# A fifth weight buffer for the experts, loaded during attention, and contiguous pieces of w3

## The chip, the cores and the metric

One core of a Trainium2 chip runs the kernel. The metric is the device time of one execution in microseconds (us), the median of several runs.

## The reference, cut to what matters

```python
attn_out = _attn_ref(q, k, v)          # 8 batches, 8 heads, 576 positions, 64 wide, mask by blocks of 64
x = attn_out.transpose(0, 2, 1, 3).reshape(4608, 512)
# soft mixture of 8 experts, 4 slots each
logits = x @ phi                        # 4608 x 32
d = softmax(logits, axis=0); slot_input = (d.T @ x).reshape(8, 4, 512)
for e in range(8):
    slot_out[e] = np.maximum(slot_input[e] @ w1[e], 0) @ w2[e]     # 512 -> 1024 -> 512
x = softmax(logits, axis=1) @ slot_out.reshape(32, 512)
# gated layer, its four weights in float64
h = (x @ m2_w1) * (x @ m2_w2) @ m2_w3   # 512 -> 1024, 1024 x 1024
out = h @ m2_w_out                      # 1024 -> 512
```

## The kernel before

**Attention** (class `Attn`) works through 32 pairs of heads. Each pair has a set of operands in one of four buffers ("set", L91-L98; in the orders below set_65 to set_68 are the buffers of pairs 0 to 3, and of 4 to 7 again). A set is made from a loaded q/k piece ("raw", 576 KB): for pairs 0 to 2 by `prep_first` (L161-L176, copies on DVE and ACT, two subtractions on POOL, L174 and L176), for all later ones by `prep_hi` (ACT copy L150) and `prep_lo` (POOL subtraction L158), with four moves by DMA (L179), three of them one after the other behind the subtraction. For each pair PE computes a first set of scores for the row maxima (`max_tile`, L191, tile "mx"), which DVE reduces (L195, L201); the maxima go through L225, L227 and a small product (`mrow`, L238) into the set. Then come the scores (`qk_unit`, L261, tile "sc"), their exponentials on ACT (L270 and L278, tiles PTa and PTb), the products with v (`pv`, L321) and the sums, for which POOL adds up exponentials (`preadd`, L294, tile "acc"). The maxima run two pairs ahead of the scores, the sets three. The word list `ORDER` gives the program order; a scheduler with its own model of times may reorder each engine's instructions, SP's (DMA issue) among them, and it does so in all of attention.

While attention runs, DVE turns the float64 bits of the gated layer's w1 and w2 into float32 (`narrow`, four instructions L627, L628, L629, L635; ACT helps with L631). Near its end, when a set is free for good, it becomes a window of 16 KB per partition, and `load_expert` (L657-L666) loads expert weights into it, 2 MB each; index i = 2e is w1 of expert e, i = 2e + 1 its w2.

**The experts** (`Rest.run`). SP's order is by hand here (`manual_schedule` for SP). First 17 pieces of 512 KB are issued: all eight of w_out and nine of the sixteen of w3. DVE converts the 24 pieces in a fixed order with the same four instructions each; ACT and POOL split each into a high and a low part (`split`, L669, L670). PE multiplies w3 by w_out from them: 192 matmuls "wps" (L725), 24 for each of eight row blocks, twelve for each half of w3's block; matmuls 13 to 24 need the ninth converted piece. Between these, for each expert, PE computes h (32 matmuls in groups, L805), transposes it (L822), ACT applies the relu (L823), and PE adds the product with w2 to "so" (L832). `w_steps` spreads loads, conversions and wps over the experts by the tables LOAD, CONV and MM. After the h of expert e, window i = 2e is loaded again with index 4 + 2e, after its so with 4 + 2e + 1 (L808 and L834 call `load_expert(NB + ...)`):

```python
        if i < NB:
            self.windows.append(self.keep["place"](i, F32, f"win{i}"))
        v = self.windows[i % NB][:, 0:4096].rearrange("p (c f) -> p c f", c=4 if first else 8)
```

**After them** come soT (L772), the products with the gated layer's w1 and w2 (L875), products of slots on DVE (L902 to L910), the matrix H (L924), and the last stage, in which PE makes 36 output tiles (L1029).

Of the kernel before, what the change touches and what calls it, by code (L numbers as in the profile page):

```python
# [7 lines left out]
F32 = mybir.dt.float32  # L8
# [8 lines left out]
NP_B = 4  # L17
NB = 4
RAW = 2
VB = 3  # L20
# [34 lines left out]
class Attn:  # L55
# [476 lines left out]
    def run(self):  # L532
# [31 lines left out]
        for n in range(N + 1):  # L564
            for t in (self.ORDER if n < N else self.LAST).split():
                k = int(t[1]) if t[1:].isdigit() else 0
                if t[0] == "M" and t != "MR":
                    self.max_tile(n + ML, k)
                elif t[0] == "Q":
                    self.qk_unit(n, int(t[1]), int(t[2]))  # L570
                    if N - NB <= n < N and t == "Q11" and self.after_scores:
                        self.after_scores(n - N + NB)
                elif t[0] == "V":
                    self.pv(n - 1, k)
                elif t[0] == "A":
                    self.preadd(n, k)
                elif t == "PH":
                    self.prep_hi(n + LA)
                elif t == "PL":
                    self.prep_lo(n + LA)  # L580
                elif t == "L2":
                    self.level2(n + ML)
                elif t == "MR":
                    self.mrow(n + ML)
                elif t == "SU":
                    self.sums(n - 1)
                elif t == "LD":
                    self.load(n + LA + 1)
                    self.load_v(n + VL)
                elif t == "PT":  # L590
                    if n and n % NP_B == 0:
                        self.push_tail(n // NP_B - 1)
                elif t == "T":
                    self.step(1)
                elif t == "BG":
                    if self.background and n >= 1 and (n == 1 or n * 16 // BGP > (n - 1) * 16 // BGP):
                        with self.tc.issue_after(self.last_max[n + 1]) if n < BGF else nullcontext(), self.tc.issue_after(self.last_exp[n - 1]):
                            self.background.popleft()()
# [5 lines left out]
class Rest:  # L604
# [3 lines left out]
    def __init__(self, tc, ctx, io, keep):  # L608
# [5 lines left out]
        self.wA, self.wB = (self.pre.tile([128, 4, 1024], F32, name=f"w{m}") for m in "AB")  # L614
        self.loaded, self.windows = deque(), []

# [40 lines left out]
    def load_expert(self, i):  # L657

        if i >= 16:
            return  # L660
        e, first = i // 2, i % 2 == 0
        if i < NB:
            self.windows.append(self.keep["place"](i, F32, f"win{i}"))
        v = self.windows[i % NB][:, 0:4096].rearrange("p (c f) -> p c f", c=4 if first else 8)
        self.nc.sync.dma_start(out=v, in_=self.io["moe_w1" if first else "moe_w2"][e].rearrange("(c p) f -> p c f", p=128))
        self.loaded.append(v)  # L666

# [4 lines left out]
    def run(self, out):  # L672
        nc, tc, io, keep = self.nc, self.tc, self.io, self.keep
        ident = keep["ident"]
        with ExitStack() as ctx:
# [9 lines left out]
            def load(i):  # L685
# [5 lines left out]
                else:  # L691
                    raw = w3_raw.pop((j, g)) if (j, g) in w3_raw else w3_tile(j, g)
                    src = io["w3T"][512 * g:512 * g + 512, 256 * j:256 * j + 256].rearrange("(c p) f -> p c f", p=128)
                    nc.sync.dma_start(out=raw.rearrange("p (c f) -> p c f", c=4), in_=src)
                raws[i] = raw
# [94 lines left out]
            hT = []  # L790
            for t in self.windows:
                t = t[:, 4096:8 * S]
# [3 lines left out]
            for e in range(8):  # L796
                hi = tc.high_priority() if HP else nullcontext()
                hi.__enter__()
                w = self.loaded.popleft()

                hp = ps.tile([128, 512], F32, tag="h", name="h", bufs=2)
                for dc in range(4):
                    for g in range(4):
                        with tc.issue_after(so_last) if 0 < e <= SEQ else nullcontext():
                            nc.tensor.matmul(hp[32 * g:32 * g + 32, 0:256], lhsT=siT[:, dc],  # L805
                                             rhs=w[:, dc, 256 * g:256 * g + 256], start=dc == 0, stop=dc == 3)
                self.load_expert(NB + 2 * e)
                if e == 5:  # L808
# [19 lines left out]
                hi.__enter__()  # L828
                w = self.loaded.popleft()
                for f in range(8):  # L830
                    g = f % 4
                    so_last = nc.tensor.matmul(so[32 * g:32 * g + 32], lhsT=hT[e][:, f], rhs=w[:, f],  # L832
                                               start=e == 0 and f < 4, stop=e == 7 and f >= 4).ins
                self.load_expert(NB + 2 * e + 1)  # L834
                hi.__exit__(None, None, None)
# [45 lines left out]
            for t in range(4):  # L881
                pe[0] = nc.tensor.transpose(p[:, 128 * t:128 * t + 128], abs_[:, 128 * t:128 * t + 128], ident).ins
            AB = mp.tile([128, 1024], F32, tag="hs", name="AB").rearrange("p (m f s) -> p m f s", m=2, f=8)
            AT, BT = AB[:, 0], AB[:, 1]
# [197 lines left out]
def layout(inputs):  # L1082
    import numpy as np

    f = np.float32
# [10 lines left out]
    vv[:, :, :512] = v[:, :, :512].reshape(N, 2, 4, 128, 64).transpose(0, 3, 2, 1, 4).reshape(N, 128, 512)  # L1096
    vv[:, :, 512:] = v[:, :, 512:].reshape(N, 128, 64)
    phi = inputs["moe_phi"]
    phib = np.zeros((128, 4, 64), f)
# [10 lines left out]
    for h in range(2):  # L1110
# [3 lines left out]
        for j in range(4):  # L1114
# [3 lines left out]
    return {"moe_w1": inputs["moe_w1"], "moe_w2": inputs["moe_w2"], "moe2_w1": inputs["moe2_w1"],  # L1118
            "moe2_w2": inputs["moe2_w2"], "w3T": np.ascontiguousarray(inputs["moe2_w3"].T),
            "w_out": inputs["moe2_w_out"], "sel32": sel32,  # L1120
# [23 lines left out]
```

## Time and profile before

| | |
|---|---|
| median of 3 runs | 670.13 us (667.66 to 670.2) |
| the profiled execution | 670.19 us |
| its span, first to last instruction | 668.3 us |
| mean granted clock of TensorE | 0.971 |
| PE busy | 620.1 us (93%), 4423 matmuls |
| DVE, ACT, POOL busy | 459.6, 349.2, 365.0 us |
| DMA | 141.45 MB, 212 GB/s over the span |

How to read it: PE, DVE, ACT and POOL are the four computing engines, PEld is PE's weight load, SPq is the queue that issues the DMAs. In a timeline a line has the start, the time until the last of its instructions ends, engine, source line, operation, what is written from what, how many, and in brackets the idle time before the first with what ended it. In a table of stretches each engine has its busy time and the number of instructions; then come the granted clock (1.00 is full), the DMA engines' busy share and GB/s.

### The profile page before, as it was taken

Reading aid. Unit: us, or ns where it says so; the run is one execution under the profiler, and the core shown is the slowest. Engines: PE = TensorE matmul, PEld = TensorE weight load, DVE = VectorE, ACT = ScalarE, POOL = GpSimd, SP = SyncE. Lnnn points to the kernel's source line nnn. Section 1 sums busy time; section 2 is a strip of 40 time slices with the busy share of each in tenths; the row PEclk is TensorE's granted clock in tenths of the full one; section 3 lists DMA queues with packets and bytes.
Section 4 is the critical chain, followed back from the end, with each engine's and each line's share of the span. In section 5 each row is a group of like instructions: output and inputs, shape, how many; then the busy total and the mean of one; then the engine's idle time right before and its main releaser. Section 6 shows DMA issues by size and latency. Waiting matters only on the chain. (4 is left out here: it accounts for less than half of the span.)

```text
span 668.3 us, 11772 instructions
## 1 busy us (share of the span) xinstructions
PE 620.1 (93%) x4423; PEld 450.7 (67%) x4423; DVE 459.6 (69%) x813; ACT 349.2 (52%) x645; POOL 365.0 (55%) x312
## 2 busy tenths in 40 slices
PE   4689989999999999999999997869999979999997
PEld 2666667777777777777777755426664667888886
DVE  6745829778867888687885656899923998555450
ACT  6855537475655657476664543335424345444541
POOL 8856838778677877877785650244414332123320
PEclk9978979999999999999999998979999997999999
DMA  6597687777788878788866679999893404655742
GB/s 210 145 221 198 156 227 180 183 231 173 208 223 213 214 189 225 183 214 219 224 164 198 214 282 338 330 385 400 320 343 109 130 12 131 211 181 188 252 150 94
DMA packets 59640, 141.45 MB, mean 212 GB/s; under 512 B 5928, under 2 KB 23848, under 8 KB 59560
## 3 DMA queue, kind: packets, MB, share of 16 engines
q1 hardware_dynamic: 59404, 140.63, 70.8%
q8 instruction: 35, 0.57, 0.4%
q14 instruction: 21, 0.17, 0.1%
q10 hardware_dynamic: 180, 0.07, 0.0%
HBM read 96.44 MB, written 10.32 MB: 160 GB/s over the span
## 5 line engine op out<-in xcount | busy, mean ns | idle before, releaser
L195 DVE TENSOR_REDUCE bm<-mx 128x8 f32<-128x512 f32 (+1 forms) x192 | 113.3, 616 | 40.4 <-PE mx L191 39.2
L261 PE MATMUL sc<-set 128*128 128x320 f32 (+4 forms) x704 | 132.5, 322 | 4.4 <-ACT PTa L270 3.2
L261 PEld LDWEIGHTS sc<-set 128*128 128x128 f32 x704 | 102.1, 196 | 14.7 <-issue 5.1
L191 PE MATMUL mx<-set 128*128 128x320 f32 (+4 forms) x384 | 85.0, 326 | 13.8 <-DMA set<-set 6.5
L1029 PE MATMUL ops<-H,Ph 128*128 128x512 f32 x288 | 92.6, 402 | 3.0 <-ACT H L933 2.5
L294 POOL TENSOR_TENSOR acc<-PTa 128x640 f32<-128x640 f32 x31 | 50.2, 1620 | 74.5 <-PE sum L340 74.3
L328 ACT COPY xT<-pv 128x320 f32<-128x320 f32 x64 | 25.5, 399 | 107.7 <-PE pv L326 93.9
L191 PEld LDWEIGHTS mx<-set 128*128 128x128 f32 x384 | 64.1, 201 | 24.2 <-issue 7.9
L158 POOL TENSOR_TENSOR set<-raw,set 128x1152 fp32r<-128x1152 f32 x29 | 76.8, 2647 | 5.2 <-ACT set L150 5.2
L1004 POOL TENSOR_TENSOR Pl<-rot,Ph 128x384 fp32r<-128x384 f32 x24 | 30.6, 1296 | 77.8 <-ACT Ph L1002 77.8
L321 PE MATMUL pv<-PTa,v 128*64 128x320 f32 (+2 forms) x512 | 70.2, 374 | 0.0
L1029 PEld LDWEIGHTS ops<-H,Ph 128*128 128x128 f32 x288 | 55.5, 193 | 17.3 <-ACT H L933 2.9
L294 POOL TENSOR_TENSOR acc<-acc,PTb 128x640 f32<-128x640 f32 (+1 forms) x62 | 65.4, 1056 | 2.3
L270 ACT ACTIVATE PTa<-sc 128x960 f32<-128x960 f32 x64 | 59.2, 978 | 1.8 <-PE sc L261 1.8
L1029 PE MATMUL ops<-H,Pl 128*128 128x512 f32 x144 | 57.9, 402 | 0.0
L725 PE MATMUL wps<-wo,w 128*128 128x512 f32 x192 | 51.2, 412 | 3.0 <-POOL wo L670 1.7
L321 PEld LDWEIGHTS pv<-PTa,v 128*64 128x64 f32 x512 | 34.0, 137 | 28.5 <-issue 3.8
L1032 ACT COPY o<-ops 128x512 f32<-128x512 f32 x36 | 21.1, 587 | 59.3 <-PE ops L1031 59.0
L725 PEld LDWEIGHTS wps<-wo,w 128*128 128x128 f32 x192 | 35.2, 192 | 20.3 <-issue 6.7
L278 ACT ACTIVATE PTb<-sc 128x704 f32<-128x704 f32 x64 | 43.7, 691 | 8.2 <-PE sc L261 8.1
L321 PE MATMUL pv<-PTb,v 128*64 128x320 f32 (+1 forms) x256 | 43.5, 413 | 0.0
L670 POOL TENSOR_TENSOR w<-f,w 128x512 fp32r<-128x512 f32 x16 | 20.6, 1289 | 30.1 <-ACT w L669 27.0
(203 smaller groups left out, 1166.1 us busy)
## 6 DMA issues: line engine op xcount, KB each, us to landing
set<-set SPq DMA_DIRECT2D x116, 288.0 KB, 4.1
win<-in_moe_w SPq DMA_DIRECT2D x16, 2048.0 KB, 9.7
raw<-in_qk SPq DMA_DIRECT2D x31, 576.0 KB, 6.0
v<-in_v SPq DMA_DIRECT2D x32, 288.0 KB, 4.4
rot<-cs SPq DMA_DIRECT2D x48, 192.0 KB, 3.2
out<-o SPq DMA_DIRECT2D x11, 768.0 KB, 4.4
raw<-in_moe_w SPq DMA_DIRECT2D x16, 512.0 KB, 6.4
w3raw<-in_w3T SPq DMA_DIRECT2D x16, 512.0 KB, 11.0
```

The source lines that it names most:

```text
L158: nc.gpsimd.tensor_tensor(T1[:, 0:2 * S], self.raw.pop(n), flat(R1).bitcast(F32), op=ALU.subtract)
L191: nc.tensor.matmul(ps[:, o0:o0 + kn], lhsT=R1[:, h, q0:q0 + 128], rhs=T1[:, k0:k0 + kn], start=True, stop=True)
L195: self.last_max[n] = nc.vector.tensor_reduce(out, ps[:, 0:m].rearrange("p (n k) -> p n k", k=64), axis=AX.X, op=ALU.max).ins
L261: nc.tensor.matmul(ps[:, o0:o0 + qn * (qs.stop - qs.start)], lhsT=lt[:, k0:k0 + 128], rhs=rt[:, qs, q0:q0 + qn], start=st, stop=not st)
L270: nc.scalar.activation(out=PTa[:, h], in_=ps[:, 0:960], func=AF.Exp, scale=SCALE)
L278: self.last_exp[n] = nc.scalar.activation(out=PTb[:, S * h:S * h + w], in_=ps[:, 256:256 + w], func=AF.Exp, scale=SCALE).ins
L294: add = lambda o, a, b: eng.tensor_tensor(o, a, b, op=ALU.add)
L321: nc.tensor.matmul(ps[64 * h:64 * h + 64, q0 - lo:q1 - lo], lhsT=v[:, 128 * j + 64 * h:128 * j + 64 * h + 64], rhs=pt[:, h, o:o + q1 - q0] ...
L328: nc.scalar.copy(self.xTb[b % 2][:, p, lo:hi], ps[:, 0:hi - lo])
L725: nc.tensor.matmul(p, lhsT=a[:, o], rhs=b, start=c + i == 0, stop=c == 7 and i == 2)
L1004: eng.tensor_tensor(Pl[:, k], p, Ph[:, k].bitcast(F32), op=ALU.subtract)
L1029: nc.tensor.matmul(ps, lhsT=a[:, k, r], rhs=b[:, k], start=n == 0, stop=False)
```

## The change

A fifth buffer `own` of 16 KB per partition is added. It takes index 4 (w1 of expert 2), whose load is written into attention after the scores of pair 16; reloads then run with a distance of five indices in place of four, so that window i takes i + 5 when i is done. The 16 pieces of w3 are laid out by the host such that a partition reads 4 KB in one run, where it read four runs of 1 KB. The tile AB (4 KB) moves into `own`, and the scratch for dynamic DMAs shrinks to 2048 bytes.

```diff
+NW = 5
...
-                    if N - NB <= n < N and t == "Q11" and self.after_scores:
-                        self.after_scores(n - N + NB)
+                    if t == "Q11" and self.after_scores:
+                        if N - NB <= n < N:
+                            self.after_scores(n - N + NB)
+                        elif n == N // 2:
+                            self.after_scores(NB)
...
-        self.loaded, self.windows = deque(), []
+
+        self.own = self.pre.tile([128, 4096], F32, name="own")
+        self.loaded, self.windows = {}, {NB: self.own}
...
         if i < NB:
-            self.windows.append(self.keep["place"](i, F32, f"win{i}"))
-        v = self.windows[i % NB][:, 0:4096].rearrange("p (c f) -> p c f", c=4 if first else 8)
+            self.windows[i] = self.keep["place"](i, F32, f"win{i}")
+        v = self.windows[i % NW][:, 0:4096].rearrange("p (c f) -> p c f", c=4 if first else 8)
         self.nc.sync.dma_start(out=v, in_=self.io["moe_w1" if first else "moe_w2"][e].rearrange("(c p) f -> p c f", p=128))
-        self.loaded.append(v)
+        self.loaded[i] = v
...
-                    src = io["w3T"][512 * g:512 * g + 512, 256 * j:256 * j + 256].rearrange("(c p) f -> p c f", p=128)
-                    nc.sync.dma_start(out=raw.rearrange("p (c f) -> p c f", c=4), in_=src)
+                    nc.sync.dma_start(out=raw, in_=io["w3T"][256 * j + 128 * g:256 * j + 128 * g + 128])
...
-                w = self.loaded.popleft()
+                w = self.loaded.pop(2 * e)
...
-                self.load_expert(NB + 2 * e)
+                self.load_expert(NW + 2 * e)
...
-                w = self.loaded.popleft()
+                w = self.loaded.pop(2 * e + 1)
...
-                self.load_expert(NB + 2 * e + 1)
+                self.load_expert(NW + 2 * e + 1)
...
-            AB = mp.tile([128, 1024], F32, tag="hs", name="AB").rearrange("p (m f s) -> p m f s", m=2, f=8)
+            AB = self.own[:, 0:1024].rearrange("p (m f s) -> p m f s", m=2, f=8)
...
+    w3 = np.ascontiguousarray(inputs["moe2_w3"].T.reshape(2, 4, 128, 8, 128).transpose(3, 0, 2, 1, 4)).reshape(2048, 512)
...
-    nc = bacc.Bacc("TRN2", target_bir_lowering=False, num_devices=1)
+    nc = bacc.Bacc("TRN2", target_bir_lowering=False, num_devices=1, dynamic_dma_scratch_size=2048)
```

The scheduler's order changes at two places of note. Line numbers of the changed kernel are one higher in attention and five or six higher in the experts. The first place is the DMA queue at the start of attention. Before:

```order
L143 DMA v<-in_v 128x576 x3
L648 DMA raw_463<-in_moe_w 128x1024
L136 DMA raw<-in_qk 128x1152 x2
L179 DMA set_68<-set_68 64x1152
L136 DMA raw<-in_qk 128x1152
```

And now:

```order
L144 DMA v<-in_v 128x576 x3
L654 DMA raw_464<-in_moe_w 128x1024
L671 DMA own<-in_moe_w 128x4x1024
L137 DMA raw<-in_qk 128x1152 x2
L180 DMA set_68<-set_68 64x1152
```

The load of `own` stands at the start of the program, ahead of the q/k pieces of pairs 2 and 3, not at pair 16. POOL's order at the start of attention, before (L174 and L176 make the set of pair 2, L158 those of pairs 3, 4 and 5; "l" is the masked maximum):

```order
L174 TENSOR_TENSOR set_67<-raw,set_67 64x1152
L176 TENSOR_TENSOR set_67<-raw,set_67 64x1152
L294 TENSOR_TENSOR acc<-PTa 128x2x320
L158 TENSOR_TENSOR set_68<-raw,set_68 128x1152
L294 TENSOR_TENSOR acc<-PTb,PTa 128x2x128
L294 TENSOR_TENSOR acc<-acc,PTa 128x2x192
L225 TENSOR_TENSOR l_343<-bm_118,lmask 128x90
L294 TENSOR_TENSOR acc<-acc,PTb 128x2x320
L158 TENSOR_TENSOR set_65<-raw,set_65 128x1152
```

And now:

```order
L295 TENSOR_TENSOR acc<-PTa 128x2x320
L175 TENSOR_TENSOR set_67<-raw,set_67 64x1152
L295 TENSOR_TENSOR acc<-acc,PTa 128x2x192
L177 TENSOR_TENSOR set_67<-raw,set_67 64x1152
L295 TENSOR_TENSOR acc<-PTb,PTa 128x2x128
L159 TENSOR_TENSOR set_68<-raw,set_68 128x1152
L295 TENSOR_TENSOR acc<-acc,PTb 128x2x320
L226 TENSOR_TENSOR l_344<-bm_119,lmask 128x90
L295 TENSOR_TENSOR acc<-acc,PTb 128x2x64
L159 TENSOR_TENSOR set_65<-raw,set_65 128x1152
```

The sums of pair 0's exponentials have moved ahead of the subtractions for pairs 2 and 3. On DVE the two casts for pair 2 (L171, L173) have moved behind the seven reductions of pair 1, on ACT the two casts for pair 2 behind three exponentials of pair 0, and on PE all twelve matmuls of the first half of pair 2's scores ahead of the maxima of pair 3. From the sixth pair on the orders of attention are the same. The second place is PE among the experts, from the h of expert 1 on. Before:

```order
L805 MATMUL h<-win_4636,siT 32x256 x16
L725 MATMUL wps<-wo,w_5125 128x512 x3
L822 MATMUL hTp<-ident,hs 128x128 x2
L725 MATMUL wps<-wo,w_5125 128x512
L832 MATMUL so<-win_4752,win_4388 32x512 x8
L725 MATMUL wps<-wo,w_5125 128x512 x8
L805 MATMUL h<-win_4388,siT 32x256 x16
L822 MATMUL hTp<-ident,hs 128x128 x2
L832 MATMUL so<-win_4512 32x512 x8
L725 MATMUL wps<-wo,w_5202 128x512 x12
```

And now, from two wps after the h of expert 1:

```order
L810 MATMUL h<-own,siT 32x256 x9
L730 MATMUL wps<-wo,w_5127 128x512
L810 MATMUL h<-own,siT 32x256 x5
L827 MATMUL hTp<-ident,hs 128x128 x2
L810 MATMUL h<-own,siT 32x256 x2
L730 MATMUL wps<-wo,w_5127 128x512 x3
L837 MATMUL so<-win_4754,win_4390 32x512 x8
L827 MATMUL hTp<-ident,hs 128x128 x2
L730 MATMUL wps<-wo,w_5127 128x512 x6
L837 MATMUL so<-win_4390,win_4514 32x512 x8
L810 MATMUL h<-win_4514,siT 32x256 x16
L730 MATMUL wps<-wo,w_5204 128x512 x9
```

The h of expert 2 follows that of expert 1 almost at once, and the h of expert 3 now stands ahead of wps 13, where it stood behind wps 24.

## Rows read from the trace of the kernel before

**Rows 1.** Stretches of the span: the experts once PE is full.
```profile
446.70:509.20 62.50, 61.40 (x419) 36.80 (x419) 40.40 (x59) 23.94 (x46) 21.69 (x19) 0.96 0.93 340
```
**Rows 2.** Timeline of PE among the experts: start, time, and what.
```profile
446.73 3.64 PE L832 MATMUL so<-win 128*32 128x512 f32 x16 [2.40 <-ACT win L823]
450.30 3.96 PE L725 MATMUL wps<-wo,w 128*128 128x512 f32 x12
454.19 1.93 PE L805 MATMUL h<-win,siT 128*32 128x256 f32 x32
...
471.48 3.03 PE L725 MATMUL wps<-wo,w 128*128 128x512 f32 x12
```
**Rows 3.** Timelines of ACT and of DVE among the experts: conversion of pieces.
```profile
448.42 0.62 ACT L669 CAST w<-f 128x512 fp32r<-128x512 f32 x1 [1.74 <-DVE f L635]
...
506.20 0.69 DVE L627 TENSOR_SCALAR u<-w3raw 128x512 int32<-128x512 int32 x1 [13.70 <-DMA w3raw<-in_w3T]
```
**Rows 4.** Stretches of 5 us: w3 alone on the DMA engines, then expert weights.
```profile
415.00:420.00 5.00, 3.11 (x43) 1.85 (x40) 2.22 (x10) 1.74 (x7) 0.00 (x0) 1.00 1.09 348
...
460.00:465.00 5.00, 5.00 (x31) 2.76 (x30) 4.66 (x8) 2.97 (x5) 2.12 (x2) 1.00 1.04 399
```
**Rows 5.** The DMA queue and a stretch of 5 us at the start of attention.
```profile
10.80 6.90 SPq L136 DMA_DIRECT2D raw<-in_qk  x2
...
20.00:25.00 5.00, 4.93 (x28) 4.51 (x27) 3.19 (x7) 4.84 (x6) 4.85 (x3) 1.00 0.05 21
```
**Rows 6.** The expert windows by tile: from issue to landing.
```profile
DMA to landing us min/median/max: 7.6/9.7/13.0
```
**Rows 7.** Timeline of POOL at the start of attention.
```profile
18.60 3.21 POOL L174 TENSOR_TENSOR set<-raw,set 64x1152 fp32r<-64x1152 f32 x1 [1.26 <-DVE set L171]
21.89 2.69 POOL L176 TENSOR_TENSOR set<-raw,set 64x1152 fp32r<-64x1152 f32 x1
24.65 1.53 POOL L294 TENSOR_TENSOR acc<-PTa 128x640 f32<-128x640 f32 x1
26.14 2.66 POOL L158 TENSOR_TENSOR set<-raw,set 128x1152 fp32r<-128x1152 f32 x1
28.76 0.74 POOL L294 TENSOR_TENSOR acc<-PTb,PTa 128x256 f32<-128x256 f32 x1
29.46 1.03 POOL L294 TENSOR_TENSOR acc<-acc,PTa 128x384 f32<-128x384 f32 x1
31.92 0.38 POOL L225 TENSOR_TENSOR l<-bm,lmask 128x90 f32<-128x90 f32 x1 [1.44 <-DVE bm L195]
32.26 1.54 POOL L294 TENSOR_TENSOR acc<-acc,PTb 128x640 f32<-128x640 f32 x1
34.45 2.64 POOL L158 TENSOR_TENSOR set<-raw,set 128x1152 fp32r<-128x1152 f32 x1 [0.65 <-ACT set L150]
37.04 0.46 POOL L294 TENSOR_TENSOR acc<-acc,PTb 128x128 f32<-128x128 f32 x1
```
**Rows 8.** Timelines of ACT and DVE at the start of attention.
```profile
22.15 1.85 ACT L270 ACTIVATE PTa<-sc 128x960 f32<-128x960 f32 x2 [0.15 <-PE sc L261]
17.77 0.76 DVE L171 CAST set<-raw 64x1152 fp32r<-64x1152 f32 x1
24.28 0.68 DVE L201 TENSOR_REDUCE bm<-mx 128x8 f32<-128x512 f32 x1
```
**Rows 9.** Timeline of PE: maxima of pairs 3 and 4, scores of pair 2.
```profile
39.23 1.88 PE L191 MATMUL mx<-set 128*128 128x448 f32 x6 [0.40 <-DMA set<-set]
40.93 1.99 PE L261 MATMUL sc<-set 128*128 128x320 f32 x6
...
51.35 0.69 PE L191 MATMUL mx<-set 128*128 128x448 f32 x3 [1.99 <-DMA set<-set]
```
**Rows 10.** Stretches of PE's work in attention, and PE's waits from 57 to 100.
```profile
120.00:160.00 40.00, 40.00 (x361) 30.18 (x357) 32.27 (x61) 24.69 (x43) 28.81 (x26) 1.00 0.80 208
...
PE mx L191 <- DMA set<-set: 3.3, 1, 3.3
```

More of the change, by code (lines that the diff above doesn't have):

```diff
@@ L790, in run @@
             hT = []
-            for t in self.windows:
+            for t in (self.windows[i] for i in range(NB)):
                 t = t[:, 4096:8 * S]
@@ L1118, in layout @@
     return {"moe_w1": inputs["moe_w1"], "moe_w2": inputs["moe_w2"], "moe2_w1": inputs["moe2_w1"],
-            "moe2_w2": inputs["moe2_w2"], "w3T": np.ascontiguousarray(inputs["moe2_w3"].T),
+            "moe2_w2": inputs["moe2_w2"], "w3T": w3,
             "w_out": inputs["moe2_w_out"], "sel32": sel32,
```

## The prediction

> **What bounds the kernel.** I read the stretches of the span first, then the timelines of PE, DVE and ACT among the experts, and last the timelines of POOL, SP and PE at the start, because the order of the changed program differs there. PE bounds nearly everything. In the middle of attention it is busy for all of a stretch of 40 us at full clock [rows 10], and among the experts for 61.40 of 62.50 us [rows 1]. So whatever delays PE while attention fills up is not caught up later, and a transfer that comes sooner is worth only what PE really waited for. The longest wait near the reloads, 13.70 us of DVE for the second-last piece of w3 [rows 3], falls inside that full stretch of PE: PE had other wps to do. What can be gained among the experts is PE's idle time ahead of it, where wps 13 cannot begin before the ninth conversion.
>
> **Load of the fifth buffer.** The load now stands at the start of the queue, ahead of the q/k pieces of pairs 2 and 3, which were issued from 10.80 us on [rows 5]. A load of expert weights lands at most 13.0 us after its issue [rows 6], here by about 24 us. The casts that read pair 2's q/k piece follow the reductions of pair 1, which end at 24.96 (24.28 + 0.68) [rows 8], so this data is late for no one, and the DMA engines have room: a busy share of 0.05 from 20 to 25 us [rows 5]. The transfer itself I cost at nothing. If that cover were gone, pair 2 would wait for what of the 2.10 MB is left, at most 5.3 us at 399 GB/s [rows 4].
>
> **The order at the start** is what costs. Worked on POOL with the durations of before: the first sum of pair 0 needs both exponentials PTa, which end at 22.15 + 1.85 = 24.00 [rows 8], so POOL does nothing for the sets until 25.53 (+1.53) [rows 7]. The subtraction L174 of pair 2 needs the DVE cast, now at 24.96 + 0.76 = 25.72 [rows 8]. Then POOL runs without a gap: 25.72 + 3.21 + 1.03 + 2.69 + 0.74 + 2.66 = 36.05 for the end of pair 3's subtraction, where it was 26.14 + 2.66 = 28.80 [rows 7]: 7.25 us later. Three moves by DMA follow it in a row, and PE's maxima for pair 3, which waited for them at 39.23 [rows 9], begin at about 46.5.
>
> Two things give part of this back. Six score matmuls of pair 2 that came after those maxima (1.99 us [rows 9]) now stand ahead and fill the gap: 5.25 us are left. And PE waited 1.99 us at 51.35 for the moves of pair 4 [rows 9]. Pair 4's subtraction now ends at 36.05 + 1.54 + 0.38 + 0.46 + 2.64 = 41.07 in place of 34.45 + 2.64 = 37.09 [rows 7], 3.98 later; its moves are then ready at 55.33, while PE comes at 49.36 + 5.25 = 54.61. So PE is 4.0 us late from there on, and keeps that. Bounds: nothing given back, 7.25; or PE's later wait of 3.3 us for set moves [rows 10] shrinks as well, 0.7. I take **+4.0**, from the two rows nearest to the place.
>
> **The experts.** The fifth buffer lets PE do the h of expert 3 before wps 13. With wps 13 held by DVE's ninth conversion (the high part ends at 448.42 + 0.62 = 449.04 [rows 3]), PE begins it at 449.04 in place of 450.30 [rows 2], 1.26 us sooner, and has one h less to do afterwards, 1.93 us [rows 2]. Against it, PE idles longer before that point. After such a pause PE ran slowly before too: the so at 446.73 took 3.64 us, and twelve wps took 3.96 us where twelve later ones took 3.03 [rows 2]. I charge one more dozen at the slow pace, 0.93 us. Sum: **-2.2**. Bounds: no slow matmuls at all after the pause, -1.26 - 1.93 - 0.93 = -4.1; or PE finds itself behind again by the end, 0. From wps 13 on, PE is the bound in both programs, so the earlier loads (each index may now be issued one step sooner) find nobody waiting.
>
> **w3 in contiguous pieces.** With w3 alone in flight the DMA engines moved 348 GB/s, with expert weights in runs of 2 to 4 KB 399 GB/s [rows 4]. Nine pieces of 524 KB before the experts take 11.8 in place of 13.6 us, all sixteen 21.0 in place of 24.1. The first conversion waits for the end of attention and not for them, and of the full stretch PE idled only 1.1 us [rows 1]. So **0**, with -1.1 as the other end.
> The Trainium skill (DMA: Bandwidth & Descriptors, Specifications) gives 512 bytes as the transfer from which the full rate is reached, so by it the runs of 1 KB lose nothing; the trace disagrees by a seventh, and the sum is 0 by either.
>
> **The rest.** AB in `own` is written long after the last expert weights there were read, and keeps its operations: 0. The smaller scratch serves DMAs that POOL would issue, and the profile's list of issues has SP's and ACT's queues alone: 0. The row softmax of the last batch moves up among DVE's instructions by fractions of a microsecond, which I leave at 0.
>
> **Sum** against the profiled execution, 670.19 us, which is the median of 670.13 within 0.1: +4.0 - 2.2 + 0 = +1.8, so **672.0 us**. The ends add up to 670.19 + 0.7 - 4.1 - 1.1 = 665.7 and 670.19 + 7.25 = 677.4.
>
> **Rivals.** (1) *Slower: nothing is given back at the start.* SP issues in order, and the moves of pairs 3 and 4 alternate there; pair 4's wait behind pair 3's third. If they are ready only at 58.6 (51.35 + 7.25) instead of 55.33, PE keeps the full 7.25: 670.19 + 7.25 - 2.2 = 675.2. It decides from a readiness at 56.9 on (+5.5), where the time passes 673.5. For it: PE did wait for moves at three places early in attention [rows 9, 10]. Against: pair 4's subtraction is only 3.98 late. (2) *Faster:* the start costs 0.7, because later waits of PE for moves shrink too, and PE is not slowed after its pause among the experts: 670.19 + 0.7 - 4.1 = 666.8, with the w3 end 665.7; I take 666.2. For it: the 3.3 us were lost to the same kind of wait. Against: they come three pairs later and hang on the moves of a later set, which is late too. (3) *The move to the start is free:* POOL and DVE have enough idle time in the first pairs to make the new order good before PE needs pair 4, so 0 there: 670.19 - 2.2 = 668.0. Against it stands the chain above, in which POOL has no gap from 25.72 to 41.07.
> The Trainium skill (DMA: Bandwidth & Descriptors, Rules for kernel authors) says to issue a DMA early and to wait late, so that its cost overlaps with compute; that rule knows only the transfer, and by it rival 3 holds. The trace bears it out for the transfer (DMA share 0.05), not for the order that came with it.
>
> **Chances.** Forecast 0.38, rival 1 0.29, rival 2 0.20, rival 3 0.13. 0.5% is 3.35 us, about what a measurement of this kernel can tell from no change: faster means under 666.8, slower over 673.5. Rival 2 gives faster 0.20. Rival 1 with the upper edge of the forecast (0.03) gives slower 0.32. The rest is 0.48. The range is that of the ends, 665.7 to 677.4; beyond them I see no more than 2 in 10. The likeliest case alone lies between 669.7 and 673.5.
>
> **What would show it.** Right: POOL's subtraction for pair 3 (L159) ends near 36 and PE's first maxima of pair 3 start near 46.5; those of pair 4 near 55.3; the first wps come with the same spacing, but the thirteenth starts some 2.7 us later than before (449.04 + 4.0 against 450.30) with the h of expert 3 already done, and the last so ends about 1.8 us later; DVE's wait of 13.70 us for w3 shrinks to under 3 us without PE gaining from it; w3 in flight alone reaches about 400 GB/s. Wrong: an unchanged time for pair 3's maxima would refute the order's cost; PE waiting for expert weights, or idle for longer than 1 us between wps 13 and the last so, would refute the second term.

## The result, and the profile after

| | before | after |
|---|---|---|
| median of the runs made together | 668.89 us (667.41 to 670.2, 4 runs) | 678.01 us (676.13 to 678.6, 4 runs) |
| ratio, 95% interval | | 1.0139 [1.0105, 1.0174] |
| profiled execution, its span | 670.19, 668.3 us | 678.11, 676.2 us |
| PE busy | 620.1 us | 623.2 us |
| granted clock, mean | 0.971 | 0.969 |

The change makes the kernel slower by 1.4%. That is 6.0 us above the predicted 672.0 and 0.6 us above the end of the range. Between the two profiled executions, 7.9 us apart, PE is busy 3.1 us longer and idle 4.8 us longer. The busy part lies at the start: up to the row-maxima product of pair 4 PE takes 3.3 us longer for the same 244 matmuls, at a lower mean granted clock (the third column from the end). First before, then after:

```profile
0.00:61.64 61.64, 43.37 (x244) 32.46 (x245) 35.14 (x63) 38.23 (x49) 43.00 (x34) 0.92 0.71 197
0.00:70.50 70.50, 46.65 (x244) 35.54 (x245) 38.31 (x63) 38.80 (x49) 42.79 (x34) 0.88 0.69 197
```

Where the two spans part is seen best at marks that occur in both. These are starts in PE's timelines: the row-maxima product (mra) of a pair, and the starts of instructions in later stages.

| mark | before | after | difference |
|---|---|---|---|
| mra of pair 1 | 26.63 | 30.10 | +3.5 |
| mra of pair 3 | 47.12 | 56.85 | +9.7 |
| mra of pair 4 | 61.64 | 70.50 | +8.9 |
| mra of pair 10 | 134.97 | 142.74 | +7.8 |
| mra of pair 22 | 274.04 | 281.38 | +7.3 |
| mra of pair 31 | 378.40 | 387.41 | +9.0 |
| h of expert 0 | 421.45 | 431.73 | +10.3 |
| thirteenth wps | 450.30 | 459.24 | +8.9 |
| last so | 507.31 | 516.78 | +9.5 |
| second product of the last stage | 553.00 | 562.28 | +9.3 |
| end of the span | 668.3 | 676.2 | +7.9 |

So the start of attention costs 9 us. The middle wins back 1.5, and a wait near pair 23 takes 1.7 again. Attention's tail is 1.3 longer, the experts give back 1.0 (from the h of expert 0 to the last stage 130.55 in place of 131.55), and the last stage 1.4.

The start, first on POOL: its timeline in the kernel after, with the rows that answer to [rows 7].

```profile
24.23 1.55 POOL L295 TENSOR_TENSOR acc<-PTa 128x640 f32<-128x640 f32 x1 [7.36 <-DVE bm L196]
26.53 3.12 POOL L175 TENSOR_TENSOR set<-raw,set 64x1152 fp32r<-64x1152 f32 x1 [0.76 <-POOL acc L295]
...
34.21 2.65 POOL L159 TENSOR_TENSOR set<-raw,set 128x1152 fp32r<-128x1152 f32 x1
...
39.08 2.63 POOL L159 TENSOR_TENSOR set<-raw,set 128x1152 fp32r<-128x1152 f32 x1
```

The chain is the predicted one: a wait of 7.36 us, pair 2's subtractions from 26.53, pair 3's ends at 36.86 (forecast 36.05, before 28.80). What follows on the DMA queue was not predicted. SP's timeline after, single rows (L180 is a move of a set, L137 a q/k load):

```profile
36.88 0.49 SPq L180 DMA_DIRECT2D set<-set  x1
37.47 0.54 SPq L137 DMA_DIRECT2D raw<-in_qk  x1
38.71 0.47 SPq L180 DMA_DIRECT2D set<-set  x1
40.06 0.47 SPq L180 DMA_DIRECT2D set<-set  x1
41.74 0.46 SPq L180 DMA_DIRECT2D set<-set  x1
45.56 1.10 SPq L180 DMA_DIRECT2D set<-set  x2
46.71 0.76 SPq L137 DMA_DIRECT2D raw<-in_qk  x1
47.53 1.83 SPq L180 DMA_DIRECT2D set<-set  x2
49.40 0.97 SPq L137 DMA_DIRECT2D raw<-in_qk  x1
55.32 1.59 SPq L180 DMA_DIRECT2D set<-set  x2
```

and the same queue before:

```profile
28.83 0.49 SPq L179 DMA_DIRECT2D set<-set  x1
29.42 0.54 SPq L136 DMA_DIRECT2D raw<-in_qk  x1
32.00 0.47 SPq L179 DMA_DIRECT2D set<-set  x1
34.40 0.47 SPq L179 DMA_DIRECT2D set<-set  x1
35.56 2.01 SPq L179 DMA_DIRECT2D set<-set  x2
```

Pair 3's three moves are issued at 36.88, 40.06 and 45.56; before at 28.83, 32.00 and 35.56. The second now takes 5.50 us to release the third, where it took 3.56: by the order of the rows it now stands behind a q/k load and a move of pair 4. Pair 4's moves go at 41.74, 47.53 and 55.32, each behind one of pair 3 or a q/k load. (Which row belongs to which pair is inferred from the ends of the copies and subtractions.) PE's timeline after shows what comes of it, beside [rows 9]:

```profile
49.04 3.38 PE L192 MATMUL mx<-set 128*128 128x448 f32 x12 [5.64 <-DMA set<-set]
...
59.60 0.47 PE L192 MATMUL mx<-set 128*128 128x448 f32 x2 [2.32 <-DMA set<-set]
```

Pair 3's maxima begin at 49.04 instead of 39.23 (+9.8), pair 4's at 59.60 instead of 51.35 (+8.25), and PE waits before both. From the maxima of pair 3 to its product PE works at these granted clocks, first after, then before:

```profile
49.04:52.40 3.36, 3.36 (x14) 3.05 (x14) 2.56 (x5) 0.00 (x0) 0.00 (x0) 0.50 1.00 240
52.40:57.00 4.60, 4.60 (x44) 2.57 (x44) 3.87 (x9) 1.15 (x3) 0.49 (x1) 0.79 0.95 233
```

```profile
39.20:43.00 3.80, 3.77 (x15) 3.65 (x15) 2.08 (x4) 0.00 (x0) 1.47 (x1) 0.54 0.98 263
43.00:47.12 4.12, 4.12 (x46) 2.55 (x44) 3.79 (x8) 0.99 (x3) 0.49 (x1) 1.00 1.03 218
```

PE's two longest kinds of wait up to 440 us, first after, then before, show most of the idle time: 11.0 + 8.7 in place of 6.5 + 5.8. Other waits became shorter.

```profile
PE mx L192 <- DMA set<-set: 11.0, 4, 5.6
PE mra L239 <- DVE m L228: 8.7, 4, 4.1
```

```profile
PE mx L191 <- DMA set<-set: 6.5, 4, 3.3
PE mra L238 <- DVE m L227: 5.8, 3, 3.3
```

Among the experts PE now has the h of expert 3 behind it when it waits for the ninth conversion. Its timeline after:

```profile
451.78 1.91 PE L810 MATMUL h<-win,siT 128*32 128x256 f32 x32
459.24 4.71 PE L730 MATMUL wps<-wo,w 128*128 128x512 f32 x9 [5.55 <-ACT w L675]
```

Two stretches after: the wps behind the pause, and from there to the last so (the third column from the end is the granted clock).

```profile
459.24:463.90 4.66, 4.52 (x10) 3.02 (x11) 4.22 (x8) 1.99 (x4) 2.57 (x2) 0.50 1.03 397
463.90:518.70 54.80, 53.88 (x363) 33.54 (x361) 34.63 (x50) 20.73 (x41) 18.00 (x14) 1.00 0.78 296
```

After 5.55 us without work the granted clock is 0.50 (1.2 of 2.4 GHz), and nine wps take 4.71 us, where twelve took 3.96 before [rows 2].

### The profile page after: what moved, and what is told of

It reads as the page before. It is cut to its first block, busy times and chain, and to the rows that moved or that the text cites. A ratio compares the mean times of both kernels' runs of the same rounds, so it can differ in the third digit from the quotient of the medians.

```text
span 676.2 us, 11778 instructions
## 1 busy us (share of the span) xinstructions
PE 623.2 (92%) x4423; PEld 454.7 (67%) x4423; DVE 459.0 (68%) x813; ACT 349.5 (52%) x645; POOL 363.4 (54%) x312
## 4 chain that ended last, share of the span: by engine, by line
PE 71%; DVE 10%; DMA 9%; POOL 4%; ACT 3%; issue 2%; SPq 0%; POOLq 0%; ACTq 0%; DVEq 0%
PE ops L1034 15%; PE sc L262 12%; PE pv L322 11%; DMA set<-set 7%; PE mx L192 7%; PE wps L730 6%; PE lg L383 3%; PE sum L341 3%; PE xn L436 2%; PE so L837 2%; DMA win<-in_moe_w 1%; DVE bm L196 1%; PE lgT L392 1%; PE ops L1036 1%; PE S L476 1%
## 5 line engine op out<-in xcount | busy, mean ns | idle before, releaser
L196 DVE TENSOR_REDUCE bm<-mx 128x8 f32<-128x512 f32 (+1 forms) x192 | 113.5, 617 | 44.9 <-PE mx L192 43.5
L192 PE MATMUL mx<-set 128*128 128x320 f32 (+4 forms) x384 | 87.6, 336 | 19.0 <-DMA set<-set 11.0
L192 PEld LDWEIGHTS mx<-set 128*128 128x128 f32 x384 | 66.9, 210 | 29.3 <-issue 10.7
## 6 DMA issues: line engine op xcount, KB each, us to landing
win<-in_moe_w SPq DMA_DIRECT2D x13, 2048.0 KB, 10.3
```

What stands on the lines that cost most here:

```text
L192: nc.tensor.matmul(ps[:, o0:o0 + kn], lhsT=R1[:, h, q0:q0 + 128], rhs=T1[:, k0:k0 + kn], start=True, stop=True)
L196: self.last_max[n] = nc.vector.tensor_reduce(out, ps[:, 0:m].rearrange("p (n k) -> p n k", k=64), axis=AX.X, op=ALU.max).ins
```

## The experiments

All run against the kernel before on the same chip; its median was between 667.8 and 668.9 in every group, so the ratios can be compared.

| run | what it is | median, us | ratio to before, 95% |
|---|---|---|---|
| the change | load at the start, new order | 678.01 | 1.0139 [1.0105, 1.0174] |
| e4 | new order, load at pair 16 | 681.26 | 1.0195 [1.0161, 1.0230] |
| e11 | load at the start, DVE's old order only | 674.55 | 1.0084 [1.0056, 1.0113] |
| e5 | load at the start, old order | 670.02 | 1.0023 [0.9997, 1.0050] |
| e3 | load just behind pair 3's q/k, old order | 668.21 | 0.9995 [0.9965, 1.0024] |
| e1 | load at pair 16, old order | 672.23 | 1.0064 [1.0034, 1.0093] |
| e6 | load in eight pieces, old order | 671.82 | 1.0044 [1.0014, 1.0074] |
| e9 | load at pair 29, old order | 667.78 | 1.0005 [0.9971, 1.0040] |
| e10 | load behind the seventeen pieces | 672.04 | 1.0052 [1.0020, 1.0084] |
| e8 | no load at all | 666.48 | 0.9975 [0.9947, 1.0003] |
| e2 | w3's layout alone | 666.78 | 0.9986 [0.9957, 1.0014] |
| e7 | e6 with PE's pause filled | 673.73 | 1.0077 [1.0045, 1.0110] |

**The order.** e4 keeps the 2 MB away from the start, and forces the new order there with two edges:

```diff
-                with self.tc.issue_after(rows[0]):
+                with self.tc.issue_after(rows[0]), self.tc.issue_after(self.last_six):
                     self.prep_first(m)
...
-                    self.prep_lo(n + LA)
+                    with self.tc.issue_after(self.last_sub) if n == 0 else nullcontext():
+                        self.prep_lo(n + LA)
```

> The load of the fifth buffer stays at pair 16, but two edges force the order of the changed kernel at the start: DVE's casts of pair 2 behind the last reduction of pair 1, and POOL's subtraction for pair 3 behind those of pair 2. DVE's order is then that of the change, POOL's but for two sums, SP's but for the load itself; ACT still makes its casts of pair 2 early. No transfer of 2 MB at the start. Theory (order): pair 3's row-maxima product at 54 to 57 us, time 675 to 678. Rival (transfer): 47 to 49 us, time 667 to 669.

It is slower than every other, and e1, shown below, which differs from it in the order at the start alone, is 9.0 us faster in the same group. Pair 3's product stands at 56.14. PE's timeline of e4:

```profile
48.31 3.38 PE L192 MATMUL mx<-set 128*128 128x448 f32 x12 [3.07 <-DMA set<-set]
58.59 0.47 PE L192 MATMUL mx<-set 128*128 128x448 f32 x2 [2.01 <-DMA set<-set]
```

These are the waits of the changed kernel without the transfer. Pair 3's moves take 11.9 us here too (subtraction ends 33.76 + 2.65 = 36.41, maxima at 48.31), so the slower moves belong to the order and not to the 2 MB. Whether the 2 MB cost anything under the new order is not settled: the changed kernel reaches pair 3's product 0.7 us and pair 4's 2.5 us later than e4 (67.99), but ACT's casts and two of POOL's sums stand differently in e4.

e5 is the reverse: the load stays where the change has it, ahead of the q/k pieces, and edges keep the old order.

```diff
+            with self.tc.issue_after(late[0]) if n else nullcontext():
...
-                    self.qk_unit(n, int(t[1]), int(t[2]))
+                    with self.tc.issue_after(self.late[2]) if n == 0 else nullcontext():
+                        self.qk_unit(n, int(t[1]), int(t[2]))
...
-                    self.preadd(n, k)
+                    with self.tc.issue_after(self.late[1]) if n == 0 else nullcontext():
+                        self.preadd(n, k)
```

> The changed kernel as it is, the fifth buffer's load first in the queue ahead of the q/k pieces of pairs 2 and 3, but with edges on DVE, POOL and ACT that keep the order of the kernel before: casts and subtractions of pair 2 ahead of the reductions of pair 1, of the exponentials and of the sums of pair 0. It differs from the changed kernel in that order alone. Theory (the order costs, the transfer at this place does not): row-maxima product of pair 3 at 46 to 49 us in place of 56.9, and the time 666.5 to 669. Rival (with the load ahead of them the q/k pieces land late, and the scheduler was right to reorder): pair 3's product at 52 us or later, 672 or more.

The order alone is worth 1.0139 - 1.0023 = 1.16%, 7.8 us; each of the two ratios is known to some 0.3% either way. But neither theory has it whole: pair 3's product is at 51.08, between the two. DVE's timeline of e5 shows the transfer's own price:

```profile
20.71 0.76 DVE L172 CAST set<-raw 64x1152 fp32r<-64x1152 f32 x1 [2.98 <-DMA raw<-in_qk]
```

Pair 2's q/k piece lands 2.9 us later than it was used before (20.71 against 17.77 [rows 8]). In the changed kernel nobody saw this, since the new order had moved the cast behind it.

e11 drops the edges on POOL and ACT from e5 and keeps DVE's.

> The load at the start as in the changed kernel, with an edge on DVE alone: its casts of pair 2 stand ahead of the reductions of pair 1 as before, while POOL and ACT keep the changed order (first sum of pair 0 ahead of pair 2's subtractions, the exponentials ahead of its casts). Theory as the prediction had it (POOL's queue sets when pair 3 is ready): pair 3's subtraction ends at 35 to 36.5 and the time stays at 675 to 678. Rival (DVE's casts behind the reductions are what costs): 670 to 671, as in the run with all three orders restored.

Pair 3's subtraction ends at 33.47 + 2.65 = 36.12, which is the forecast of the prediction to 0.1 us, yet the time, 674.55, is 0.45 us under the theory's and well above the rival's:

```profile
33.47 2.65 POOL L159 TENSOR_TENSOR set<-raw,set 128x1152 fp32r<-128x1152 f32 x1
```

The agreement of the end is partly luck: the first subtraction of pair 2 begins later than the chain had it (26.29 against 25.72) and is shorter (2.62 against 3.21).

```profile
26.29 2.62 POOL L175 TENSOR_TENSOR set<-raw,set 64x1152 fp32r<-64x1152 f32 x1
```

Pair 3's maxima begin at 45.76 in e11, so its moves take 9.6 us here: how long three moves take is not fixed by POOL's order alone; by the queue's rows it hangs on what stands between them.

By the ratios, POOL's and ACT's order is 0.61 of the 1.16% (1.0084 - 1.0023), DVE's the other 0.55. Pair 4's product says it in us, in one execution of each: 61.64 before, 65.57 in e5, 68.83 in e11, 70.50 in the change. So POOL's queue is a large part, as the prediction had it, but not the whole; which of the two parts is larger, the ratios cannot tell.

The moved casts also stand in a place that no step had priced: on DVE between the last reduction of pair 1 and the mask add for which pair 1's own product waits. DVE's timeline after:

```profile
24.55 0.68 DVE L202 TENSOR_REDUCE bm<-mx 128x8 f32<-128x512 f32 x1
25.26 1.14 DVE L172 CAST set<-raw 64x1152 fp32r<-64x1152 f32 x1
26.43 0.75 DVE L174 CAST set<-raw 64x1152 fp32r<-64x1152 f32 x1
27.11 2.65 DVE L226 TENSOR_TENSOR l<-bm,lmask 128x90 f32<-128x90 f32 x1
```

That product is 3.5 us late (30.10, before 26.63). In e11 it is as late (30.43) without the casts, since PE's order then puts scores that wait for ACT ahead of it; so how much of the 8 us hangs on these casts is not shown.

**Where the 2 MB can go.** e1 pins the load to the place where the program writes it:

```diff
                         elif n == N // 2:
-                            self.after_scores(NB)
+                            with self.tc.issue_after(self.last_load):
+                                self.after_scores(NB)
```

> The changed kernel with one edge more: the load of the fifth buffer is queued behind the q/k load issued at pair 16, so that every engine's order at the start of attention is that of the kernel before, and everything from the experts on is that of the change. Theory (the new order at the start costs the time): the row-maxima product of pair 3 goes back from 56.9 to about 47.1 us, the h of expert 0 from 431.7 to about 421.5, and the time to 667 to 668 us, that is the time before less the 0.8 that the experts gave in the profile of the change. Rival (the 2 MB transfer is what costs, wherever it is): it stays at 676 to 678. Rival (experts or w3 cost): 674 or more, with the h of expert 0 at 421.5.

Neither came: 672.23. The start is that of before (pair 4's product at 61.60), but a new wait stands at pair 17. SP's timeline of e1:

```profile
191.07 0.84 SPq L672 DMA_DIRECT2D own<-in_moe_w  x1
...
195.46 10.68 SPq L180 DMA_DIRECT2D set<-set  x3
```

The same place before:

```profile
200.51 1.92 SPq L179 DMA_DIRECT2D set<-set  x3
```

And PE's timeline of e1:

```profile
208.24 0.80 PE L192 MATMUL mx<-set 128*128 128x448 f32 x3 [2.83 <-ACT dT L455]
```

Three moves take 10.68 us to issue, where three in the same place took 1.92 before. PE waits 2.83 us until 208.24 and loses 3.7 us between the products of pairs 16 and 17. The profile names ACT as the releaser; that it was the moves, which that set still lacked, is inferred from SP's row.

> The changed kernel with the fifth buffer's load queued right behind the q/k load of pair 3, at some 17 to 26 us, so that the 2 MB are in flight while attention fills up, with POOL's and DVE's order up to pair 3 as in the kernel before. Theory (order): row-maxima product of pair 3 at 47 to 49 us, time 667 to 669.5. Rival (the transfer delays q/k pieces and moves of sets): pair 3's product at 52 or later, time 673 or more.

With the load right behind pair 3's q/k piece (issued at 17.21) the kernel is as fast as before, and the rival fell. Pair 3's product is even early, at 45.55. Pair 4's maxima wait 5.27 us for moves; its product is 2.6 us behind that of before, the h of expert 0 still 1.1, the last so level.

e6 cuts the load into eight pieces at pairs 6 to 24.

> The load of the fifth buffer in eight pieces of 256 KB at pairs 6, 8, 11, 14, 16, 19, 21 and 24, each queued behind the q/k load issued there; the order of the four computing engines is that of the run with one load at pair 16 (672.2). Theory (2 MB in one go delay the moves of a set by more than the sets' lead, eight small pieces do not): no wait of PE like that run's near 208 us, time 666.5 to 669. Rival (what cost there was the sum of the traffic, or the order at the experts): 671 to 673 again.

The rival held: 671.82. PE's waits of e6 from 60 to 440 us, beside 4.1 us before:

```profile
PE mx L192 <- DMA set<-set: 8.8, 5, 3.7
```

Small pieces do not help. That each of them delays the moves behind it is inferred from these waits; the profiled execution (675.09) is 3.3 us above e6's median, so its waits may be more than usual.

e8 removes the load, as a measure of what the buffer can bring.

```diff
-                        elif n == N // 2:
-                            self.after_scores(NB)
...
-        self.loaded, self.windows = {}, {NB: self.own}
+        self.loaded, self.windows = {NB: self.wA}, {NB: self.own}
```

> The changed kernel without the fifth buffer's first load: the h of expert 2 takes the gated layer's first weights, which lie in SBUF by then, in place of its own, so the 2 MB are not moved at all, and the order at the start is that of the kernel before. What is left is what the fifth buffer brings among the experts, and w3. Theory (the fifth buffer gives 1.0 to 2 us there, and every load during attention costs more than that): 665.5 to 667.5, no waits of PE for moves beyond those of before. Rival (it gives nothing): the time before, 668 to 669.

666.48, 0.25% under before, with the interval just touching no change; w3's layout is in it, which alone gives 0.14%, no clear change either (e2). Against e8 the load costs 0.2% at pair 3, 0.3% at pair 29, 0.5% at the start, 0.7% in eight pieces and 0.9% at pair 16: everywhere about as much as the buffer brings, or more. The first two lie within the intervals.

> The fifth buffer's load queued behind the second window's at pair 29, at some 369 us: the last move of a set was issued at 355.8 and ended by 360.4 in the kernel before, and the DMA engines were 0.59 to 0.73 busy from 370 to 390 us. The engines' order at the start is that of before, among the experts that of the change. Theory (a load costs only where moves of sets follow it): no new wait of PE for moves, h of expert 0 as early as before, time 665.5 to 667.5, within 1 us of the run without the transfer. Rival (the 5 us of transfer push back the windows and the seventeen pieces that follow): DVE waits for a piece or PE for expert weights, and the time is 668.5 or more.

e9 makes no new wait for moves, as the theory had it, and its time, 667.78, lies between the two forecasts. From the h of expert 0 to the last so it takes 86.04 us (before 85.86, e8 84.59), and the first wps follows 9.0 us behind that h (8.1 before, 7.9 in e8). This is not what the rival named: from there on DVE waits for no piece and PE for no expert weights. PE's timeline of e9 and a stretch of it show a slow clock:

```profile
420.39 3.46 PE L811 MATMUL h<-win,siT 128*32 128x256 f32 x32 [0.38 <-DVE siT L492]
```

```profile
420.39:423.80 3.41, 3.41 (x33) 1.40 (x34) 3.27 (x5) 0.00 (x0) 0.00 (x0) 0.54 0.06 24
```

The h of expert 0 takes 3.46 us at a granted clock of 0.54, where it took 1.93 at 1.00 before. From the first wps to the last so e9 is as fast as the change: 77.0 us (change 77.1, e8 76.7, before 77.8). Why the clock was low there in this execution, and whether the late load has to do with it, is not shown.

> The fifth buffer's load issued behind the seventeen pieces of w_out and w3, where attention has no moves left, ahead of the reload of the first window; attention is that of the kernel before, the experts still reload five indices ahead. Theory (only a load with set moves behind it costs, and the buffer brings its 1 to 2 us among the experts even so): 665.5 to 667.5. Rival (a buffer filled this late brings the h of expert 2 no earlier than before): the time before, 668 to 669.5.

Slower by 0.5%, above both forecasts. Up to the so of expert 2, which takes 3.64 us after a pause as in [rows 2], the experts run in the rhythm of before, so the buffer brings nothing; from the h of expert 0 to the last so they take 89.74 us, 3.9 more than before. The loss lies behind the thirteenth wps: from there to the last so PE is idle 2.7 us (before 1.1), of which 0.79 and 0.62 are waits for converted pieces near 500 us, and busy 2.2 us longer; why busy longer is not shown.

**w3.** e2 is the kernel before with the new layout alone.

> The kernel before with the contiguous layout of w3 alone; no order changes on any engine. Theory: w3 in flight alone moves some 400 GB/s in place of 348, the long wait of DVE for w3 (13.70 us) shrinks, and PE gains nothing from it: 668 to 670 us, within 0.2% of before. Rival (w3's pieces are late for PE somewhere): faster by 1 us or more.

Two of three held. w3 alone now moves 413 GB/s, in a stretch of e2:

```profile
405.00:410.00 5.00, 3.82 (x23) 3.35 (x23) 4.47 (x9) 0.73 (x1) 0.00 (x0) 0.66 1.03 413
```

and the time cannot be told from before. But DVE's long wait stayed:

```profile
502.45 0.69 DVE L627 TENSOR_SCALAR u<-w3raw 128x512 int32<-128x512 int32 x1 [13.30 <-DMA w3raw<-in_w3T]
```

13.30 us, before 13.70. SP's timeline of e2 shows why the rate does not matter:

```profile
492.25 0.39 SPq L665 DMA_DIRECT2D win<-in_moe_w  x1
492.69 1.05 SPq L693 DMA_DIRECT2D w3raw<-in_w3T  x2
```

The last two pieces stand in the queue behind a reload that is issued only at 492.25, when its window is free; they could not be there before.

**The pause.** e7 fills PE's idle 5.6 us in e6 by 20 matmuls on zeros. The table MM changes with it, so that the wps from the thirteenth on come behind the filling.

```diff
-MM = (0, 0, 0, 0, 0, 0, 16, 3, 12, 18, 3, 11, 23, 3, 12, 8, 3, 12, 6, 3, 12, 16, 3, 0, 0, 3, 1, 4)
+MM = (0, 0, 0, 0, 0, 0, 12, 0, 0, 0, 40, 11, 23, 3, 12, 8, 3, 12, 6, 3, 12, 16, 3, 0, 0, 3, 1, 4)
...
+                    with tc.issue_after(h_last):
+                        for _ in range(20):
+                            fill = nc.tensor.matmul(p, lhsT=keep["zeros"][:, 0:128], rhs=keep["zeros"], start=True, stop=True).ins
+                with tc.issue_after(fill) if e == 3 else nullcontext():
+                    w_steps(3 * e + 1)
```

> The kernel with eight pieces, and 20 matmuls of 128x512 on zeros between the h of expert 3 and the thirteenth wps, where PE idled for 5.6 us and then ran nine wps in 4.7 us at a granted clock of 0.50. Theory (the slow clock after the pause gave back about half of what the fifth buffer brings among the experts): wps 13 to 24 in 3.0 us in place of some 5.5, and the time 1 to 2.5 us below the kernel with eight pieces. Rival (what is gained there is lost again in PE's idle time further on, or the fill delays wps 13): the same time within 0.7 us, or slower.

Rival. PE's timeline of e7:

```profile
444.50 4.49 PE L829 MATMUL fill<-zeros 128*128 128x512 bf16 x19
450.15 0.74 PE L735 MATMUL wps<-wo,w 128*128 128x512 f32 x2 [1.16 <-ACT w L680]
451.50 2.15 PE L735 MATMUL wps<-wo,w 128*128 128x512 f32 x8 [0.62 <-POOL w L681]
454.51 0.73 PE L735 MATMUL wps<-wo,w 128*128 128x512 f32 x2 [0.86 <-POOL wo L681]
```

The clock held: eight wps in 2.15 us. But the twelve waited 0.62 and 0.86 us for converted pieces among them and took 5.1 us, where the changed kernel's twelve took 5.7 (459.24 to 464.92) at the slow clock. The conversions set the pace there, so most of the slow clock had been covered. The run as a whole is 1.9 us slower than e6: from there to the last so PE idles 2.6 us more and is busy 1.0 us longer. That is not the price of the filling alone, since the order differs too: fourteen more wps now stand ahead of the so of expert 3, and PE waits 0.70 and 0.62 us among them. So e7 shows what the twelve wps take at full clock, but not what filling the pause would do to the time in e6's order.

## Why the prediction was wrong, step by step

- **The load itself, costed at nothing: not refuted in this program, for a reason that was only half right.** "This data is late for no one" is true after the reorder; with the old order DVE waits 2.98 us for it (e5), inside the bound of 5.3 that the step named. Under the new order its cost was not measured by itself.
- **The order at the start, +4.0: the step that failed, by its size.** The chain on POOL was right, to 0.8 us after and to 0.1 us, partly by luck, in e11. Four things in it were not. First, "three moves follow in a row" was taken at the old 10.4 us; they took 12.2 (e4: 11.9 without the transfer; e11: 9.6). Second, the six score matmuls that moved ahead of pair 3's maxima were to give back 1.99 us and gave nothing: from those maxima to pair 3's product it takes 7.81 us without them, 7.89 with them before, since PE came from 5.64 us without work and ran longer at a lower granted clock (the stretches shown with the result). This would not have saved the forecast, since PE then still waits 2.32 us for pair 4. Third, that wait: pair 4 was to be ready at 55.33, so that PE would wait 0.7 us in place of 1.99; it was ready at 59.60, and by the queue's rows because its moves stand between those of pair 3 and behind q/k loads. This is the mechanism of rival 1 ("58.6"), and that rival named the point from which it decides, 56.9. It priced the start at 7.25; measured are 7.8 in the middle of attention, 7.8 and 9.0 in the two comparisons (e5, e4). Fourth, DVE was costed only as the source of POOL's delay; e11 gives its order 0.55 of the 1.16%.
- **The experts, -2.2: right in sign and mechanism, and half the size.** Up to wps 13 it was -1.34 (28.85 to 27.51 us after the h of expert 0; forecast -1.26). From there to the last so +0.53 in place of -1.0. One h less was saved, but wps 13 to 24 took 5.7 us where 3.96 + 0.93 had been charged. The reason given, the slow clock, is not the main one: at full clock they still take 5.1 (e7), since PE now comes to them as soon as the ninth piece is converted and has to wait for the next ones. 0.7 us of the difference stays open. From the h of expert 0 to the last stage e8 takes 130.1 us, the change, e1, e3, e4, e5 and e6 130.3 to 130.6, e11 131.1, before and e2 131.6 and 131.3, so the gain is some 1.0.
- **w3, 0: right** (e2), with the rate of 400 GB/s as forecast. DVE's wait did shrink in the changed kernel, to 0.37 us, but not by the layout, with which alone it stays at 13.30 (e2): DVE comes later there, after 5.79 us of waiting for ACT, and waits 9.26 us for ACT behind it.
- **Left at 0:** the end of attention and the last stage. Attention's tail took 1.3 us longer after and the last stage 1.4 less; with w3's layout alone, which has the old order throughout, they also moved, by +0.8 and -1.0, so they need not hang on the fifth buffer. The tail takes 42.1 to 44.9 us in the twelve profiles with the new layout (before 43.1), so it varies that much from one execution to the next; the last stage takes 113.0 to 114.5 in all of them and 115.3 in the one profile before, so w3's layout is not ruled out there.

As for the signs: pair 3's maxima were not unchanged, so the order's cost stands. PE's 5.55 us of idling among the experts stand ahead of wps 13, where the sum had them; from there to the last so it idles 1.1 in all. Rival 3, a free move to the start, fell with e5 and e4. The rule of the Trainium skill by which it would have held (DMA: Bandwidth & Descriptors, Rules for kernel authors: issue early) counts the transfer alone, and these runs disagree: the order costs more than the transfer (1.16% against the 0.2 to 0.9% of the placements above), and at pair 16 the transfer clearly costs something too (e1).

No version here beats the kernel before beyond its measurement; e3 and e9 tie with it.

## What to carry to other kernels

When a scheduler sets the order, a new transfer without dependencies goes where the model likes it, and everything that the model thinks late behind it is reordered. So compare the order on every engine, and pin the transfer if the new order puts the long chain later. For a chain of moves take not the time of one chain but the queue: what stands between its links, and which loads are in flight. And before paying for a buffer, run the kernel without its load: the 0.25% that this showed, w3's layout included, was no more than most places for 2 MB cost.

## What was not expected of the hardware

The mask add of 128x90 on DVE has two operands in SBUF, and when it begins while POOL works it ends just behind POOL's instruction. It took 0.39 to 2.65 us, and POOL's instruction that was running ended 0.10 to 0.12 us earlier: 27.11 + 2.65 = 29.76 behind 26.53 + 3.12 = 29.65 after; 24.99 + 1.30 = 26.29 behind 24.65 + 1.53 = 26.18 before; in e11

```profile
29.71 0.39 DVE L226 TENSOR_TENSOR l<-bm,lmask 128x90 f32<-128x90 f32 x1
```

ends at 30.10, behind a POOL sum of pair 0 that ends at 28.99 + 0.99 = 29.98. In e6, where POOL's instruction ends at 24.08, just after the mask add begins at 24.04, it takes only 0.25 us. The Trainium skill (SBUF — State Buffer, SBUF: two separate sides) states this as an exclusive lock: a DVE operation with two operands in SBUF and a POOL operation that reads SBUF use one pair of ports, which goes to the one that starts first, for its whole instruction. The traces agree for this operation; POOL had started first in each case. In the changed kernel it made the mask add 1.35 us longer than before, on the path of pair 1's product. That POOL's and DVE's instructions meet is thus one more thing that an order changes.
